# Two transformer layers in one kernel: the first norm in two halves, Q per token tile, two filler banks at the start, wo and w2 loaded later, a margin behind spreads, and the last chunk's waits filled

## The chip, the cores and the metric

The kernel runs on one core of one Trainium2 chip. The core has five engines that run on their own instruction streams and meet through semaphores: TensorE (PE, matrix products into the PSUM banks), VectorE (DVE), ScalarE (ACT), GpSimd (POOL) and SyncE (SP, which here only starts transfers). Each engine takes its own instructions strictly in the order of the program. The metric is the device time of one execution in microseconds (us), lower is better. The time before is the median of three runs, and one more execution was profiled.

## The reference

`x` is 2048 tokens by 512 features in bf16. Two layers are computed, each with the same weights: a block of attention with 32 heads of 16 features, then a dense block with 1792 hidden features.

```python
def _A_ref(x, wqkv, wo):
    B, S, D = x.shape
    H = 32
    Dh = D // H
    qkv = (x @ wqkv).reshape(B, S, 3, H, Dh) ...
    scores = jnp.einsum("bhqd,bhkd->bhqk", q, k) * (Dh ** -0.5)
    p = _softmax(scores, axis=-1)
    o = jnp.einsum("bhqk,bhkd->bhqd", p, v)
    return o ... @ wo

def _B_ref(x, w1, w2):
    h = jnp.einsum("bsd,df->bsf", x, w1)
    h = jnp.maximum(h, zero)
    return jnp.einsum("bsf,fd->bsd", h, w2)

x = A_x
x = x + _A_ref(_layernorm(x, axis=-1), A_wqkv, A_wo)
x = x + _B_ref(_layernorm(x, axis=-1), B_w1, B_w2)
x = x + _A_ref(_layernorm(x, axis=-1), A_wqkv, A_wo)
x = x + _B_ref(_layernorm(x, axis=-1), B_w1, B_w2)
```

## The kernel before, in words

**Tiles.** Tokens are held in 16 tiles of 128 (`x_t`), four to a chunk of 512 queries (`QS`, `TPC`). Heads go in eight groups `t` of four heads, two of them (`e` = 0, 1) to one weight tile `T`. The scores of one head, one key block of 128 (`kb`) and one chunk of queries are one unit: 128 x 512 numbers, one PSUM bank.

**Slots.** The main loop (`while units`) takes three units at a time into the three banks of `ps_s[0]` or `ps_s[1]` in turn. One such step is a slot: three score products on PE (L1583), one exponential on ACT over two or three banks (L1596) into one of five buffers `e`, and later the products with V into `ps_o` (`pv`, L1124). Where the third unit goes to DVE, a piecewise linear stand-in for the exponential is made of one pass per unit (`lin`, L1239) and, for every three such units (a "pair" in the code, `GROUP` = 3), two or three quick passes (`up`, `down`, L1291, L1296). The two together share the work of the softmax; the choice for each slot is made when the program is written, by the conditions in front of `half, take = 0, sg`: room in the buffers, the state of the fillers (`pace`, `press()`), and in the first layer whether V 15 is made, with at most three pairs at a time before that.

**Fillers.** All other products (K, V, Q, the output projection `o`, the dense block's `h` and `z`) are groups in the queues `urgent` and `work`. They run on PE between the slots into one bank, `ps_f` (L511), and DVE empties it (`put_evac`, `do_evac`). `bank_free` is the time at which the bank is free; `fill_pe` starts a group only when nothing waits to be emptied. `owed` and `pace` say how many units of filler a slot may take.

**The order is written out by hand.** The program keeps an estimated clock of PE and DVE in ns (`now_pe`, `now_dve`), of the ends of the exponentials (`exp_end`), of SP's queue (`sp_free`, `sp_lag`) and of POOL (`pool_free`). Every result has an estimated date (`made`, `mark`, `at`), and instructions are put into each engine's stream in the order of these dates. The chip then waits by semaphores for what is really needed. If something comes later than its date, what stands behind it on the same engine waits too.

**The start.** Loads of `x` go out on SP and ACT, of the Q and K weights on SP, ACT and POOL into `stage` (which lies in the later home of `w2`), and are interleaved into `wkq`: T=0 and T=1 by ACT, T=2 and 3 by POOL (L199). 24 idle matmuls (L1317) run on PE. The first four tiles are normed in one go: `ln_stats` (L547), `ln_root` (a reciprocal root by DVE, L568 to L590), `ln_apply` (L598), transposes on PE (L607) and copies (L1345). K, Q and V 0 of the first tile are full-width products (`plain`, L1355), Q is masked into `qbuf` by one DVE pass (L756). `wo` (L224) and `w2` (L1363) are loaded on SP at once, ahead of the DMA transposes of the later chunks (L646), whose landing is dated `CROWDED` = 4500 ns later in the first layer.

**The sums.** A segment of PV products ends in `finish_segment`: DVE copies `ps_o` out (L1016, L1018), SP gathers the row of sums into `c` (L1023), DVE takes reciprocals (L1074), SP scatters them back (L1077) and, except at a chunk's end, POOL's queue spreads them over partitions (L1079); then one product gives `ot`.

**The end.** After the last slot come what is left of PV, the last chunk's projection (L1658), the rest of its `h` groups, a copy of `x` by ACT (L1672), norm, transposes, a copy of `xnT` (L1711), the second-to-last chunk's part of the dense product (`half_part`), the last chunk's dense block (L1749, L1751) and the copy and store of the last tile (L1764, L1765).

```python
need_by = exp_end[no - 1] - MM - PE_TO_ACT
limit = max(need_by - 60.0, s_ready) - SWITCH
...
mark(("c", n, e), lag=sp_lag(SMALL))
```

## Time and profile before

| | us |
|---|---|
| median of three runs | 1464.91 |
| the three runs | 1463.79, 1464.91, 1469.01 |
| the profiled execution | 1468.29 |
| its span, first to last instruction | 1466.5 |
| ACT busy in it | 1431.8 |
| DVE busy in it | 1303.0 |
| PE busy in it | 1373.3 |
| mean granted clock of PE | 0.997 |

The page names engines PE, PEld (weight loads, beside PE), DVE, ACT, POOL and SP; "SPq" and "POOLq" rows are instructions that only start transfers. L12 is line 12 of the kernel. A row of the timeline gives the start, the time from the first to the last of a run of like instructions, engine, line, operation, output and inputs, their number, and in brackets the idle time of the engine before it and what ended that. A row of the groups gives busy time and mean ns of one, then the idle time before. A row of the windows gives the stretch and its length, the busy time of each engine with its instructions, the granted clock, the DMA engines' busy share and GB/s. PE's rows are modelled at their ends, and PE is also given repeated score products to keep it streaming, so its busy share does not say how full it is.

### The profile page before, as it was taken

The page shows a single profiled execution, that of the slowest core. Times are in us where ns is not written, and L with a number is a line of the kernel's source. Part 1 is how long each engine was busy: PE and PEld are TensorE (multiplying, and loading weights), DVE is VectorE, ACT ScalarE, POOL GpSimd, SP SyncE. Part 2 cuts the span into 40 slices and gives each one's busy share as a digit, 9 for nine tenths or more (in the row PEclk, how much of TensorE's full clock was granted, in tenths as well). Part 3 has the DMA queues.
Part 4 walks back from the last instruction along what each step waited for, and adds up shares of the span by engine and source line. Part 5 has one row for each costly group of instructions (what it writes and reads, how often), then busy time and mean ns, then how long its engine had stood idle before and what let it go on. Part 6 is the DMA issues. An engine that isn't in the chain of part 4 may idle for free.

```text
span 1466.5 us, 47730 instructions
## 1 busy us (share of the span) xinstructions
PE 1373.3 (94%) x21066; PEld 511.0 (35%) x21070; DVE 1303.0 (89%) x2409; ACT 1431.8 (98%) x1390; POOL 93.3 (6%) x244
## 2 busy tenths in 40 slices
PE   8899899999999999999899999899999999999998
PEld 3232222222232223322223233223234444545665
DVE  7879999999999999999699977899989599898883
ACT  7999899999999999999999999999999999999996
POOL 4000000001010010000000000001001010010000
PEclk9999899999999999999999999999999999999999
DMA  7101000111012010120100100001111210323120
GB/s 205 19 5 24 18 17 16 42 28 31 10 31 46 13 27 10 38 46 17 24 5 23 34 9 5 11 14 24 39 36 23 46 31 24 72 47 73 21 49 19
DMA packets 135152, 46.59 MB, mean 32 GB/s; under 512 B 119808, under 2 KB 132160, under 8 KB 134944
## 3 DMA queue, kind: packets, MB, share of 16 engines
q1 hardware_dynamic: 128032, 37.47, 10.9%
q0 software_dynamic: 5568, 5.15, 1.9%
q8 instruction: 164, 2.69, 0.8%
q10 hardware_dynamic: 1344, 0.92, 0.2%
q14 instruction: 44, 0.36, 0.1%
HBM read 24.38 MB, written 2.10 MB: 18 GB/s over the span
## 4 chain that ended last, share of the span: by engine, by line
ACT 73%; PE 18%; DVE 6%; issue 2%; DMA 2%; SPq 0%; POOL 0%; DVEq 0%; ACTq 0%
ACT e L1596 72%; PE ps_s L1583 6%; PE ps_f L511 6%; PE ps_o L1124 5%; DVE lin L1239 2%; PE ps_s L1658 1%; DMA wv<-in_A_wqkv_dram 1%; DVE up L1291 0%; DVE down L1291 0%; DMA c<-ht 0%; SPq L224 0%; DVE ht L833 0%; DMA w<-in_B_w_dram 0%; DVE x L872 0%; DVE vaug L742 0%
## 5 line engine op out<-in xcount | busy, mean ns | idle before, releaser
L1596 ACT ACTIVATE e<-ps_s 128x1024 bf16<-128x1024 f32 (+1 forms) x1366 | 1420.3, 1214 | 11.8 <-PE ps_s L1583 9.4
L1239 DVE TENSOR_SCALAR lin<-ps_s 128x512 int16<-128x512 f32 x987 | 659.2, 685 | 42.6 <-PE ps_s L1583 37.0
L1583 PE MATMUL ps_s<-q,ktp 32*128 32x512 bf16 (+2 forms) x6241 | 580.0, 325 | 48.3 <-ACT e L1596 41.3
L1124 PE MATMUL ps_o<-e,vaug 128*32 128x512 bf16 (+2 forms) x4324 | 402.1, 327 | 11.9 <-DVE u L1018 4.4
L1583 PEld LDWEIGHTS <-ktp 32*128 32x128 bf16 x6241 | 183.2, 91 | 520.2 <-issue 503.8
L1124 PEld LDWEIGHTS <-vaug 128*32 128x32 bf16 x7150 | 178.5, 95 | 236.2 <-issue 205.1
L1291 DVE TENSOR_SCALAR up<-lin 128x1536 int16<-128x1536 int16 x329 | 181.2, 551 | 10.1 <-PE ps_o L1124 9.3
L1291 DVE TENSOR_SCALAR down<-lin 128x1536 int16<-128x1536 int16 x329 | 181.4, 552 | 2.0 <-PE ps_o L1124 1.9
L1124 PE MATMUL ps_o<-up,vaug 128*32 128x512 bf16 (+2 forms) x1308 | 170.1, 329 | 0.0
L1124 PE MATMUL ps_o<-lin,vaug 128*32 128x512 bf16 (+2 forms) x1308 | 155.5, 328 | 2.2 <-DVE ktp L993 1.0
L1124 PE MATMUL ps_o<-down,vscaled 128*32 128x512 bf16 (+2 forms) x1098 | 142.6, 335 | 3.3 <-DVE down L1291 2.9
L511 PE MATMUL ps_f<-xnT,w 128*32 128x512 bf16 (+2 forms) x2080 | 135.2, 343 | 5.0 <-DVE ht L833 3.8
L511 PE MATMUL ps_f<-w,ht 128*32 128x512 bf16 x1680 | 128.9, 382 | 0.9 <-DVE ht L833 0.5
L511 PE MATMUL ps_f<-xnT,wkq 128*32 128x512 bf16 (+2 forms) x1376 | 99.2, 352 | 7.6 <-DVE ktp L706 1.6
L833 DVE TENSOR_SCALAR ht<-ps_f 128x512 bf16<-128x512 f32 (+1 forms) x108 | 73.0, 676 | 23.8 <-PE ps_f L511 23.7
L511 PEld LDWEIGHTS <-w 128*32 128x32 bf16 x2080 | 46.9, 95 | 43.6 <-issue 33.8
L1124 PEld LDWEIGHTS <-vscaled 128*32 128x32 bf16 x1098 | 45.9, 96 | 19.1 <-issue 13.0
L511 PEld LDWEIGHTS <-ht 128*32 128x32 bf16 x1680 | 37.0, 95 | 40.0 <-issue 25.4
L511 PEld LDWEIGHTS <-wkq 128*32 128x32 bf16 x1376 | 32.4, 95 | 39.9 <-issue 31.7
L547 DVE BATCH_NORM_STATS2 stats<-x 128x6 f32<-128x512 bf16 x64 | 42.7, 684 | 2.5 <-ACT x L1672 1.1
L511 PE MATMUL ps_f<-wv,xnT 128*32 128x512 bf16 x496 | 37.7, 382 | 5.7 <-DVE vaug L742 2.2
L511 PE MATMUL ps_f<-wo,ot 128*32 128x512 bf16 x496 | 39.7, 382 | 0.8 <-DVE x L794 0.5
(139 smaller groups left out, 537.8 us busy)
## 6 DMA issues: line engine op xcount, KB each, us to landing
w<-in_B_w_dram SPq DMA_DIRECT2D x130, 128.0 KB
q<-xn SPq DMA_DIRECT2D x48, 64.0 KB
out_dram<-x SPq DMA_DIRECT2D x16, 128.0 KB
x<-in_A_x_dram SPq DMA_DIRECT2D x14, 128.0 KB
w<-in_B_w_dram SPq DMA_DIRECT2D x1, 1792.0 KB
u<-r POOLq DMA_DIRECT2D x12, 128.0 KB, 4.5
ktp<-in_B_w_dram SPq DMA_DIRECT2D x10, 128.0 KB
u<-ht POOLq DMA_DIRECT2D x6, 128.0 KB, 4.5
```

The source lines that it names most:

```text
L511: nc.tensor.matmul(out[cols], lhsT[:, cols], rhs, start=i % k == 0, stop=i % k == k - 1, tile_position=(0, 32 * g), skip_group_check=True,)
L547: nc.vector.bn_stats(out=stats[ln_n(tag)][:, i, :], in_=x_t[tt][:])
L833: nc.vector.tensor_scalar(out=out, in0=sums, scalar1=0.0, scalar2=None, op0=ALU.max)
L1124: nc.tensor.matmul(ps_o[32 * g : 32 * g + 32, 0 : sg["w"]], values[:, 4 * sg["T"] + g, 2 * e : 2 * e + 32], rhs, start=g not in sg["begun" ...
L1239: first = nc.vector.tensor_scalar(out=lin[which][:, half * QS : (half + 1) * QS], in0=src, scalar1=EXP_BIAS, scalar2=0.0, op0=ALU.add, op1 ...
L1291: nc.vector.tensor_scalar(out=out, in0=line, scalar1=by, scalar2=0.0, op0=ALU.add, op1=ALU.max)
L1583: score = nc.tensor.matmul(b[:, a : a + sg["w"]], kt[32 * g : 32 * g + 32, kc : kc + P], qbuf[sg["n"] % 2][32 * g : 32 * g + 32, sg["e"], ...
L1596: ex = nc.scalar.activation(out=eb[:, 0 : place[m]], in_=b[:, 0 : place[m]], func=ACTF.Exp, scale=1.0 / (LOG2E * UNIT),)
L1658: uses(nc.tensor.matmul(out, lhsT, rhs, start=first, stop=last), b, needs=needs)
```

## The change

- **Norm and Q at the start.** The first norm runs in two halves of two tiles; the root is one power on POOL per half, the same form that the end of the kernel uses. The transposed tiles go to fixed banks. K is made for 128 and then for 384 columns, Q by tile of 128 tokens into one bank, its masks by two passes. The idle matmuls are 13, then 4 and 3 between the halves. V 0 becomes a filler like V 1 to 3.
- **Weights.** Of the interleaves of T=0 and T=1 all but Q's T=0 move from ACT to POOL. `wo` and `w2` wait in a queue `to_load` and go out one per slot from slot 30, when the estimate has SP free, `w2` in 14 pieces. Dates are written in for `wkq`, `wv` and the tiles of `x`, and groups and statistics depend on them.
- **Two filler banks.** Until the first PV product `ps_o` serves as a second bank for fillers, and PV starts once `BOTH` = 4 exponentials are pending and no filler is open.
- **Margins.** The landing of `c` is dated `BEHIND` = 3500 ns later while a spread is under way. `CROWDED` holds only before 18000 ns. The estimated clocks start 2760 ns (PE) and 3100 ns (DVE) sooner.
- **The end.** Before the last PV, fillers and PV are placed in the waits for the last two exponentials. Statistics of the last tile are read from PSUM beside ACT's copy. The transposes go to `ps_o`'s bank first, `xnT` is copied by DVE and ACT in halves, and the last tile is copied and stored in halves on two queues.

```diff
-    CROWDED, POOL_ISSUE = 4500.0, 700.0
+    CROWDED, POOL_ISSUE, BEHIND = 4500.0, 700.0, 3500.0
+    LOADED, FIRST_LOAD = 18000.0, 30
+    BOTH = 4
+    X_AT = (9.9, 10.1, 11.0, 11.4, 11.6, 11.9, 12.2, 12.5, 13.5, 14.5, 15.0, 15.5)
+    WQ_AT, WV_AT = {0: 0.0, 1: 12500.0, 2: 16500.0, 3: 17900.0}, 9900.0
...
+    to_load = deque()
     for T in range(NDC):
         for e in range(2):
             rows = A_wo[T * P : (T + 1) * P, :].rearrange("(g e d) f -> e g d f", g=4, e=2)
-            nc.sync.dma_start(out=wo[1 - e : P : 2, T, :], in_=rows[e])
+            to_load.append((wo[1 - e : P : 2, T, :], rows[e]))
+    for ft in range(NF):
+        to_load.append((w2[:, ft, :], B_w2[ft * P : (ft + 1) * P, :]))
...
+    def next_bank():
+
+        if not two[0] or any(e[3] == 1 for e in evac):
+            return 0
+        if any(e[3] == 0 for e in evac):
+            return 1
+        return int(bank_free[1] < bank_free[0])
+
     def start_group(g):
         (urgent if g in urgent else work).remove(g)
-        ready = max(at(g["deps"], "pe"), bank_free[0] + DVE_TO_PE)
+        now_bank[0] = next_bank()
+        ready = max(at(g["deps"], "pe"), bank_free[now_bank[0]] + DVE_TO_PE)
...
-                if evac:
+                if len(evac) > two[0]:
                     return
...
-                lag = sp_lag(TRANSPOSE) + (0.0 if l else CROWDED)
+                lag = sp_lag(TRANSPOSE) + (CROWDED if now_dve[0] < LOADED else 0.0)
...
-                mark(("c", n, e), lag=sp_lag(SMALL))
+                behind = BEHIND if now_dve[0] < spread_till[0] else 0.0
+                mark(("c", n, e), lag=sp_lag(SMALL) + behind)
...
                 lag = max(pool_free[0] - now_dve[0] + SPREAD_LAG, R_LAG)
+                spread_till[0] = now_dve[0] + lag
...
+            if two[0] and (len(pend) < BOTH or cur or evac):
+                break
...
-    idle_matmuls(24)
+    idle_matmuls(13)
...
+    for n in range(2):
+        rows = range(n * HALF, (n + 1) * HALF)
+        for i in rows:
+            ln_stats(tag, i, i)
+        for i in rows:
+            nc.vector.bn_aggr(out=mv[0][:, i, :], in_=stats[0][:, i, :])
+        nc.vector.tensor_scalar(
+            out=half_va[n][:], in0=mv[0][:, rows.start : rows.stop, 1], scalar1=EPS, scalar2=None,
+            op0=ALU.add,
+        )
+        nc.gpsimd.tensor_tensor(
+            out=half_ya[n][:], in0=half_va[n][:], in1=masks[:, 4:5].to_broadcast((P, HALF)),
+            op=ALU.pow,
+        )
+        set_ones(*((8, 13), (13, 16))[n])
+    interleave(nc.gpsimd.tensor_copy, 0, 0)
+    interleave(nc.gpsimd.tensor_copy, 0, 1)
+    set_ones(16, len(ones))
+    interleave(nc.gpsimd.tensor_copy, 1, 1)
...
+    for n in range(2):
+        for i in range(n * HALF, (n + 1) * HALF):
+            head_apply(i)
+        for i in range(n * HALF, (n + 1) * HALF):
+            head_transpose(i)
+        idle_matmuls((4, 3)[n])
+    interleave(nc.scalar.copy, 1, 0)
+    head_k(0, P, (2, 0))
     for i in range(TPC):
...
+        head_q(i)
+    head_k(P, QS, (0, 1))
...
-    now_pe[0] = 13160.0
-    now_dve[0] = 14500.0
-    exp_end = {-1: 12600.0, 0: 13600.0}
+    now_pe[0] = 10400.0
+    now_dve[0] = 11400.0
+    exp_end = {-1: 9900.0, 0: 10900.0}
+    pool_free[0] = WQ_AT[3]
+    sp_free[0] = 15500.0
...
+        if to_load and no >= FIRST_LOAD and sp_free[0] < now_pe[0]:
+            out, in_ = to_load.popleft()
+            nc.sync.dma_start(out=out, in_=in_)
+            sp_lag(W1, "pe")
+    assert not to_load
+    owed[0] = 99.0
+    for limit in (exp_end[slot[0] - 1], exp_end[slot[0]]):
+        fill_v(limit, 1)
+        fill_pe(limit + ACT_TO_PE)
...
-    more = [(last, w) for w in range(W)] + [(3, 0)]
+    more = [(3, 0)] + [(last, w) for w in range(W)]
...
+        uses(
+            nc.vector.bn_stats(out=stats[ln_n(tag)][:, i, :], in_=at_bank(banks[i])), banks[i], "x"
+        )
         uses(nc.scalar.copy(out=x_t[tt + i][:], in_=at_bank(banks[i])), banks[i], "x")
...
-        copy = nc.vector.tensor_copy if i % 2 else nc.scalar.copy
-        uses(copy(out=xnT[NQS - 1][:, :, part(i)], in_=pt), more[i], "xnT")
+        for n, copy in enumerate((nc.vector.tensor_copy, nc.scalar.copy)):
+            cs = slice(n * NDC // 2, (n + 1) * NDC // 2)
+            uses(copy(out=xnT[NQS - 1][:, cs, part(i)], in_=pt[:, cs]), more[i], "xnT")
...
+        for copy, queue, a in ((nc.scalar.copy, nc.scalar, 0), (nc.vector.tensor_copy, nc.sync, D // 2)):
+            cols = slice(a, a + D // 2)
+            uses(copy(out=x_t[tt + i][:, cols], in_=at_bank(banks[i])[:, cols]), banks[i])
+            queue.dma_start(
+                out=out_flat[(tt + i) * P : (tt + i + 1) * P, cols], in_=x_t[tt + i][:, cols]
+            )
```

143 lines of the change are left out of this document (82 added, 61 removed).

## The prediction

> **What bounds the kernel now.** I read the page first, then ACT's waits, then three stretches of the timeline: the start, the one long gap of ACT, the end.
>
> ```profile
> span 1466.5 us, 47730 instructions
> PE 1373.3 (94%) x21066; PEld 511.0 (35%) x21070; DVE 1303.0 (89%) x2409; ACT 1431.8 (98%) x1390; POOL 93.3 (6%) x244
> ...
> L1596 ACT ACTIVATE e<-ps_s 128x1024 bf16<-128x1024 f32 x987 | 931.3, 1097 | 7.6 <-PE ps_s L1583 5.7 <-PE ps_o L1124 0.7
> L1596 ACT ACTIVATE e<-ps_s 128x1536 bf16<-128x1536 f32 x378 | 530.7, 1519 | 4.2 <-PE ps_s L1583 3.6 <-PE ps_o L1124 0.2
> ```
>
> ACT is busy for 98% of the span, nearly all in the exponentials of L1596. There are 987 + 378 + 1 = 1366 slots, one ACTIVATE each. The idle column holds 11.8 us in all. A slot takes three score blocks of 512 columns, and in 987 of them DVE takes the third, so ACT reads 1024 columns and not 1536. The two mean times differ by 0.422 us: a block more for DVE saves ACT that much. So four things can change the time: when the first exponential starts, gaps between exponentials, the number of DVE blocks, and what follows the last exponential.
>
> The start (timeline, 0 to 25 us, and SP's next row after it):
>
> ```profile
> 1.18 8.27 PE L1317 MATMUL ps_o<-e 128*128 128x512 bf16 x24 [1.18 <-DVE e L207]
> 3.31 2.47 DVE L547 BATCH_NORM_STATS2 stats<-x 128x6 f32<-128x512 bf16 x4 [0.92 <-DMA x<-in_A_x_dram]
> 5.70 0.36 DVE L568 BATCH_NORM_AGGREGATE mv<-stats 128x2 f32<-128x6 f32 x4
> 7.13 1.83 PEld L1317 LDWEIGHTS <-e 128*128 128x128 bf16 x9 [0.28 <-issue]
> 7.58 1.39 ACT L199 COPY wkq<-w 128x512 bf16<-128x512 bf16 x2 [4.43 <-DMA w<-in_A_wqkv_dram]
> 8.20 1.38 DVE L598 TENSOR_SCALAR xn<-x,mv,ya 128x512 bf16<-128x512 bf16 x4
> 10.59 0.86 DVE L1345 COPY xnT<-ps_s 128x512 bf16<-128x512 bf16 x2 [1.01 <-PE ps_s L607]
> 11.60 1.89 PE L1355 MATMUL ps_s<-xnT,wkq 128*128 128x512 bf16 x7 [0.18 <-DVE xnT L1345]
> 13.53 1.23 DVE L756 TENSOR_TENSOR q<-ps_s,masks 128x1024 bf16<-128x1024 f32 x1 [0.88 <-PE ps_s L1355]
> 15.24 1.45 ACT L1596 ACTIVATE e<-ps_s 128x1536 bf16<-128x1536 f32 x1 [0.72 <-PE ps_s L1583]
> 19.58 1.07 POOL L564 TENSOR_TENSOR ya<-va,masks 128x4 f32<-128x4 f32 x1
> 23.93 24.60 SPq L646 DMA_TRANSPOSE xnT<-xn  x12
> ...
> 97.09 1.19 SPq L779 DMA_DIRECT2D q<-xn  x2
> ```
>
> Four statistics, a reciprocal root by DVE steps (6.1 to 8.2), four scalings, transposes, K, Q, its masks and the first scores stand in one chain of 15.24 us. On SP twelve transposes follow, and nothing from 48.5 to 97.
>
> The long gap (timeline, 141 to 160 us, and windows):
>
> ```profile
> 141.44 1.38 POOL L1079 DMA_DIRECT2D u<-ht  x2 [110.31 <-DVE ht L1016]
> 141.94 0.59 SPq L1023 DMA_DIRECT2D c<-ht  x1
> 147.22 0.35 DVE L1074 RECIPROCAL c<-c 128x32 f32<-128x32 f32 x1 [3.01 <-DMA c<-ht]
> 148.04 0.61 PE L1124 MATMUL ps_o<-down,vscaled 128*32 128x512 bf16 x3 [2.87 <-DVE down L1291]
> 149.67 1.02 ACT L1596 ACTIVATE e<-ps_s 128x1024 bf16<-128x1024 f32 x1 [2.90 <-PE ps_s L1583]
> ...
> 156.81 43.85 ACT L1596 ACTIVATE e<-ps_s 128x1024 bf16<-128x1024 f32 x44 [0.49 <-PE ps_s L1583]
> ...
> 140.00:160.00 20.00, 16.27 (x139) 3.59 (x138) 14.70 (x27) 15.08 (x16) 2.60 (x4) 0.74 0.22 43
> ```
>
> The 8 KB copy of the sums was issued 0.5 us after two 128 KB spreads on POOL's queue, and its RECIPROCAL started 5.3 us after the issue. DVE takes its work in order, so it stood 3.0 us before the reciprocal; behind it stood `down`, for that PE, and for PE ACT 2.9 us. Then the granted clock falls (0.74 over the window) and ACT waits 0.49 to 0.50 us before each of the next slots. In this window ACT is busy 15.08 of 20: 4.9 us lost.
>
> **The change, part by part.**
>
> *First norm.* The order written out: statistics of tiles 0, 1, their aggregate and eps, statistics of 2, 3, the same; the root is one POW on POOL per half; DVE's nine small steps go. From the rows: 3.31 + 2.47 + 0.36 + two eps steps (some 0.3 each with their gaps) = 6.75. The second POW ends at about 7.6: 1.07 for four columns here, 0.57 for one (end, below), I take 0.75 for two. Tiles 0 and 1 are scaled in that wait, 2 and 3 by 8.35, against 9.58 before: 1.2 us sooner. Ahead of the POWs on POOL stand eight memsets, and the K weights of T=0 follow behind them (copy 0.7, as ACT's 1.39 for two), ready at about 8.7, before the first K needs them.
>
> *Q per token tile.* Transposes to 9.3 with four idle matmuls between the pairs, last copy (0.43) to 9.8. K of the first 128 columns, Q by 16 matmuls of 128 columns, K of the other 384: the row of seven 512-column matmuls gives 0.27 each; 128 columns cost 0.07 by width and 0.14 if weight loads limit, so Q 1.1 to 2.2. Half masks follow (half of 1.23). First scores wait for the first mask only, but the copy of K's 384 columns (about 0.5) stands ahead of the first exponential on ACT. That gives 12.6 to 13.7; I take 13.1, a gain of 2.1. Bounds: 1.5 from the slow end, and 2.8, the distance between the start times that the scheduler is given (13160 and 10400 ns).
>
> *Weights of T=1.* Two ACT copies (1.38, done before 15.24) go to POOL, which the program waits for by a date; 0 on ACT.
>
> *Idle matmuls.* Row 7.13: the loads come after an idle of 0.28 up to there (0.43 apart with the load's own 0.15), and nine in 1.83 us from there, 0.20 apart, so the first 13 end at about 6.8, with 0.4 us to the first transpose. The Trainium skill (TensorE: Matmul & The Clock Gate, "Part 1: The HAM clock gate") says that the array starts at half clock and is released after a busy window of about 3.4 us which runs free of the kernel. By it thirteen are enough, unless the window falls badly; the trace agrees in kind (0.43, then 0.20) and shows the change of pace 5.9 us after the first matmul.
>
> *Loads moved.* SP loses eight wo issues and the 1.8 MB w2 before the transposes, so w1 and the transposes meet an emptier queue; 22 smaller issues come one per slot from slot 30. SP is free from 48.5 to 97.09, and slots 30 to 60 fall in about 50 to 90; the 22, at the 0.6 of the copy of 141.94, are 13 us of that: 0. With the cover gone each late transpose would cost at most its own 0.6.
>
> *Two filler banks, first PV held until four exponentials are pending, transposes believed sooner.* Here is the supply of DVE blocks.
>
> ```profile
> 20.00:40.00 20.00, 16.74 (x215) 5.15 (x211) 13.30 (x25) 19.30 (x15) 6.28 (x19) 1.00 0.80 186
> ...
> 70.00:80.00 10.00, 1.96 (x3) 1.00 0.01 2
> ...
> 102.92 0.79 DVE L742 CAST vaug<-ps_f 128x512 bf16<-128x512 f32 x1 [2.01 <-PE ps_f L511]
> ...
> 110.00:120.00 10.00, 7.55 (x12) 1.00 0.01 2
> ```
>
> (The 10 us windows are of L1239 alone.) Before the sixteenth V is evacuated, at 103.7, pairs are held to three at a time, 3 blocks in 10 us; after it, 12. Sooner V brings the fast stretch forward. But the bank lasts only until the first PV, some five slots, and the norms of chunks 1 to 3 wait for POOL as before (its clock starts at 17900 for them), so I expect V 15 some 4 us sooner beside the shift of the start, and 3 blocks more: 1.3 us. Ends: 3 blocks fewer (-1.3) and 10 more (4.2). The held PV is made up in PE's 3.3 us of slack in 20 to 40.
>
> *Margin behind spreads.* The reciprocal is planned 3.5 us later when a spread is under way. 5.3 us after the issue is 5.9 after the DVE step that released it; the planned lag becomes about 0.2 + 0.6 + 1.45 + 3.5 = 5.75. What is left of the wait is 0.1, and what DVE does instead is ready work. The gap goes: 4.8. Late next is the spread, which has the 10 us of its own date. Ends: 0, if it returns elsewhere, and 4.9.
>
> *The end* (timeline, 1429 us on, and one early row for a price; the last exponential ends at 1429.73 + 16.87 = 1446.6):
>
> ```profile
> 35.52 0.69 DVE L706 CAST ktp<-ps_f 128x512 bf16<-128x512 f32 x1 [0.48 <-PE ps_f L511]
> ...
> 1429.73 16.87 ACT L1596 ACTIVATE e<-ps_s 128x1536 bf16<-128x1536 f32 x13
> 1442.96 0.42 DVE L833 TENSOR_SCALAR ht<-ps_f 128x256 bf16<-128x256 f32 x1
> 1449.24 0.59 ACT L1672 CAST x<-ps_s 128x512 bf16<-128x512 f32 x1 [2.64 <-PE ps_s L1658]
> 1449.86 0.69 DVE L547 BATCH_NORM_STATS2 stats<-x 128x6 f32<-128x512 bf16 x1 [1.10 <-ACT x L1672]
> 1451.03 0.57 POOL L1699 TENSOR_TENSOR ya<-va,masks 128x1 f32<-128x1 f32 x1 [24.67 <-DVE va L1695]
> 1452.48 0.38 PE L607 MATMUL ps_s<-ident,xn 128*128 128x128 bf16 x4 [0.48 <-ACT ht L831]
> 1452.91 3.19 PE L1658 MATMUL ps_s<-w,ht 128*128 128x512 bf16 x14
> 1462.85 0.59 ACT L1764 CAST x<-ps_s 128x512 bf16<-128x512 f32 x1 [0.63 <-PE ps_s L1658]
> 1463.46 0.33 SPq L1765 DMA_DIRECT2D out_dram<-x  x1
> ```
>
> Statistics straight from PSUM drop the copy from the chain: 0.6, if they read PSUM as fast (DVE's 512-column read of PSUM in row 35.52 takes 0.69, as the statistics from SBUF do here). The transposes' own bank drops the wait for `ht`, 0.48. But four `h` groups also run in that wait, and PE takes them first: filled earlier, the whole 1.1 is had; left there, 0.5. The halved xnT copy is worthless while the fourteen matmuls of 1452.91 stand ahead on PE. The last copy in halves: 0.59 to 0.42, two queues: 0.2. Sum 1.0 to 1.3, or 0.5 at the low end; I take 1.2.
>
> **Sum.** 2.1 + 1.3 + 4.8 + 1.2 = 9.4 us. The profiled execution took 1468.29 (span 1466.5 and 1.8 around it); less 9.4 is 1458.9. The median of the runs is 1464.91 (1463.79, 1464.91, 1469.01): less 9.4 is 1455.5. Part of the 3.4 between them may be the gap itself, smaller in some runs; the order of the two queues that makes it is fixed by the program, so I stay near the second: 1456.
>
> **Rivals.**
>
> *The gap is moved, or small in the unprofiled runs.* For it: two runs at 1464, two at 1469, about a gap apart; every slot is laid out anew, and the next spread can catch another transfer. Against it: the margin holds wherever a spread is dated. Then 9.4 - 4.8 = 4.6 remain: 1460.3. Chance 0.25.
>
> *The array stays slow in the head.* If the gap between the thirteen matmuls and the transposes spoils the release, the head's PE work of some 2.5 us doubles: 1458.5. This is the rule of the skill read against the change; the row of 7.13 speaks against it, as the release falls only 0.3 after the thirteenth. Chance 0.07.
>
> *DVE blocks lost* (the other side).
>
> ```profile
> 700.00:720.00 20.00, 17.17 (x220) 5.67 (x216) 9.41 (x19) 20.00 (x17) 1.33 (x3) 1.00 0.15 28
> 720.00:740.00 20.00, 18.86 (x223) 6.12 (x222) 18.60 (x38) 20.00 (x21) 0.00 (x0) 1.00 0.05 16
> ```
>
> The scheduler's gates on the backlog close at times: DVE drops to 9.41 of 20, and ACT gets 17 slots through, not 21: 4 slots, 3.8 us. All gates stand on the same estimated clock, which the change moves. More such droughts eat the gain: the 9.4 are gone at 22 blocks lost (22 x 0.422), and four droughts more (15 us) give 1470.5. For it: such droughts exist before. Against it: nothing in the change adds DVE work after the head. Chance 0.1.
>
> *Blocks won.* V early and one drought less, 15 blocks more than my three: 6.3 us, 1450. For it: DVE is busy 13.3 of 20 in row 20:40. Against it: two fillers at once last five slots. Chance 0.13.
>
> **How the numbers follow.** Forecast 0.45, rivals 0.25, 0.07, 0.1, 0.13. 0.5% is 7.3 us, about what a measurement of this kernel can tell from no change, so the line to faster is 1457.6. The forecast's own range, 1452.5 to 1459.5 by the ends above, lies some three quarters below it: 0.34, with the blocks won 0.13, and of the moved gap and the slow array, whose prices spread over 3 us, about 0.07: faster 0.54. Slower needs over 1472: 0.07, within the fourth rival's spread. Same 0.39. The range reaches to the moved gap and into the lost blocks above, and to the blocks won below: 1449 to 1465.
>
> **What would show it.** First exponential at 13.1 (not below 12.4, not above 13.7). Granted clock 1.00 and ACT 20 of 20 throughout 120 to 180. V 15 evacuated before 98. The count of 1024-column exponentials 987 to 997. From the last exponential's end to the last store's issue 15.7 where 16.8 stood. The forecast is wrong if a new gap of ACT above 1 us appears, if the count falls under 975, or if the gap of 149.67 turns up under another transfer.

## The result and the profile after

The changed kernel took 1457.13 us, the median of 4 runs (1456.49 to 1457.35), against 1465.74 of the kernel before run beside it (1463.79 to 1469.01). The ratio is 0.9938, 95% interval [0.9919, 0.9957]: 8.6 us less, where 9.4 had been forecast and 1456 named. The profiled execution of the changed kernel took 1457.35 us. The page's first lines:

```profile
span 1455.5 us, 47936 instructions
PE 1367.1 (94%) x21143; PEld 508.9 (35%) x21143; DVE 1310.0 (90%) x2421; ACT 1424.9 (98%) x1389; POOL 97.0 (7%) x249
```

The groups of ACT's exponentials, by form (count, then total and mean, then the idle time ahead of them):

```profile
L1678 ACT ACTIVATE e<-ps_s 128x1024 bf16<-128x1024 f32 x996 | 938.8, 1098 | 3.1 <-PE ps_s L1665 1.6 <-PE ps_o L1144 0.8
L1678 ACT ACTIVATE e<-ps_s 128x1536 bf16<-128x1536 f32 x369 | 520.2, 1514 | 3.2 <-PE ps_s L1665 2.0 <-PE ps_o L1144 0.5
```

Nine blocks more went to DVE (996 for 987), and the idle time ahead of the exponentials fell from 11.8 to 6.3 us. Third, ACT's rows of the timeline and the window that held the long gap:

```profile
14.00 4.26 ACT L1678 ACTIVATE e<-ps_s 128x1536 bf16<-128x1536 f32 x3 [0.19 <-PE ps_s L1665]
...
21.62 661.25 ACT L1678 ACTIVATE e<-ps_s 128x1536 bf16<-128x1536 f32 x655 [0.35 <-PE ps_o L1144]
...
1418.78 16.75 ACT L1678 ACTIVATE e<-ps_s 128x1536 bf16<-128x1536 f32 x13 [0.40 <-PE ps_s L1665]
```

```profile
140.00:160.00 20.00, 17.82 (x206) 5.68 (x202) 19.20 (x37) 20.00 (x21) 1.38 (x2) 1.00 0.11 22
```

The first exponential starts at 14.00 instead of 15.24. From 21.62 on, 655 exponentials stand in one row, without a gap that the view would split; ACT is busy 20.00 of 20 between 140 and 160, at a granted clock of 1.00. The last one ends at 1418.78 + 16.75 = 1435.53, and the span ends 19.97 later.

So the difference of the two spans, 11.0 us, splits like this:

| | before | after | less by |
|---|---|---|---|
| first exponential starts | 15.24 | 14.00 | 1.24 |
| ACT idle between exponentials (first start to last end, less their busy time) | 11.1 | 6.0 | 5.0 |
| exponentials, busy | 1420.3 | 1415.5 | 4.8 |
| last exponential's end to the span's end | 19.9 | 19.97 | -0.07 |

The profiled execution of before was one of its longer ones (1468.29; the runs begin at 1463.79), so these 11.0 us hold 2.4 more than the medians do. Which parts of the change the rows belong to is what the experiments had to say.

### The profile page after: what moved, and what is told of

The parts are those of the page before. It is cut to its first block, busy times and chain, and to the rows that moved or that the text cites. A ratio compares the mean times of both kernels' runs of the same rounds, so it can differ in the third digit from the quotient of the medians.

```text
span 1455.5 us, 47936 instructions
## 1 busy us (share of the span) xinstructions
PE 1367.1 (94%) x21143; PEld 508.9 (35%) x21143; DVE 1310.0 (90%) x2421; ACT 1424.9 (98%) x1389; POOL 97.0 (7%) x249
## 4 chain that ended last, share of the span: by engine, by line
ACT 70%; PE 21%; DVE 7%; issue 2%; DMA 1%; POOL 0%; DVEq 0%; ACTq 0%; SPq 0%
ACT e L1678 70%; PE ps_f L526 7%; PE ps_s L1665 7%; PE ps_o L1144 6%; DVE lin L1264 2%; PE ps_s L1749 1%; DVE up L1316 1%; DVE down L1316 0%; DVE ht L851 0%; DVE x L890 0%; DVE stats L562 0%; DVE down L1321 0%; DVE xn L1390 0%; PE ps_f L622 0%; DVE vaug L758 0%
## 5 line engine op out<-in xcount | busy, mean ns | idle before, releaser
L1678 ACT ACTIVATE e<-ps_s 128x1024 bf16<-128x1024 f32 (+1 forms) x1366 | 1415.5, 1210 | 6.3 <-PE ps_s L1665 3.6
L526 PE MATMUL ps_f<-xnT,wkq 128*32 128x512 bf16 (+2 forms) x1376 | 96.0, 353 | 5.2 <-DVE ht L851 1.3
L571 POOL TENSOR_TENSOR ta<-stats 128x4 f32<-128x4 f32 (+2 forms) x17 | 4.7, 275 | 575.5 <-DVE stats L562 575.5
```

The lines of the kernel that those rows point to most:

```text
L526: nc.tensor.matmul(out[cols], lhsT[:, cols], rhs, start=i % k == 0, stop=i % k == k - 1, tile_position=(0, 32 * g), skip_group_check=True,)
L571: pool.tensor_tensor(out=t1, in0=st[:, :, 1], in1=st[:, :, 4], op=ALU.subtract)
L1678: ex = nc.scalar.activation(out=eb[:, 0 : place[m]], in_=b[:, 0 : place[m]], func=ACTF.Exp, scale=1.0 / (LOG2E * UNIT),)
```

## The experiments

Each is an edit of the changed kernel unless it says otherwise. Several chips were used, on which the kernel before had medians of 1464.77 to 1467.10, so parts are compared by their ratio to the kernel before run beside them; 0.001 is 1.47 us. Each ratio is known to 0.001 to 0.002, so a difference of two ratios below some 0.002 (3 us) isn't clear of noise by itself; where a part is smaller than that, the rows of its traces have to show it.

### The start: POOL beside the scalings

The first exponential came 0.9 later than the 13.1 forecast. The timeline of the changed kernel, 6 to 11 us:

```profile
6.61 0.73 DVE L1390 TENSOR_SCALAR xn<-x,mv,half_ya 128x512 bf16<-128x512 bf16 x2
6.78 0.79 POOL L1373 TENSOR_TENSOR half_ya<-half_va,masks 128x2 f32<-128x2 f32 x1 [0.39 <-DVE half_va L1369]
...
7.61 2.81 DVE L1390 TENSOR_SCALAR xn<-x,mv,half_ya 128x512 bf16<-128x512 bf16 x2 [0.27 <-POOL half_ya L1373]
...
7.71 1.52 POOL L203 COPY wkq<-w 128x512 bf16<-128x512 bf16 x2
...
9.13 1.13 POOL L239 MEMSET vaug<- 128x32 bf16 x12
...
10.48 0.40 PE L622 MATMUL ps_s<-ident,xn 128*128 128x128 bf16 x4 [1.41 <-DVE xn L1390]
```

The statistics and both POWs came as forecast (0.73 and 0.79 for the 0.75 taken). But the second pair of scalings took 2.81 us where the first took 0.73, and it ran beside two copies and twelve memsets of POOL. In the kernel before POOL's memsets ended at 6.55 and the scalings began at 8.20. The last transposes waited 1.41 us for it. The experiment holds POOL back until the scalings are done, by a copy of one column of `xnbuf[3]`:

```diff
-    interleave(nc.gpsimd.tensor_copy, 0, 0)
-    interleave(nc.gpsimd.tensor_copy, 0, 1)
-    set_ones(16, len(ones))
...
         idle_matmuls((4, 3)[n])
+    nc.gpsimd.tensor_copy(out=warm[:], in_=xnbuf[TPC - 1][:, 0:1])
+    interleave(nc.gpsimd.tensor_copy, 0, 1)
+    interleave(nc.gpsimd.tensor_copy, 1, 1)
+    set_ones(16, len(ones))
...
+    interleave(nc.scalar.copy, 0, 0)
     interleave(nc.scalar.copy, 1, 0)
```

> The changed kernel, with POOL's copies and the last twelve memsets held until the fourth scaling (a one-column POOL copy that reads it), and K's T=0 weights interleaved by ACT after its two transposed copies. Theory (the third and fourth scalings of the first norm took 1.00 and 1.89 us in the changed kernel, where two others took 0.37, because POOL's copies and memsets ran beside them): all four scalings 0.35 to 0.45 us, first exponential at 12.7 to 13.2 us where it was 14.00, time about 1456.0 (1.1 us less). Rival (what stretched them is something else, such as the loads that land at 350 GB/s): scalings stay at 1.0 and 1.9, and the first exponential comes at 14.0 to 14.7, later for the copy given to ACT.

Measured: 1456.06 us (1455.41 to 1456.25, 4 runs), ratio 0.9935 [0.992, 0.995]. Its timeline:

```profile
7.47 0.36 POOL L239 MEMSET vaug<- 128x32 bf16 x3
7.55 0.74 DVE L1382 TENSOR_SCALAR xn<-x,mv,half_ya 128x512 bf16<-128x512 bf16 x2 [0.27 <-POOL half_ya L1373]
...
12.29 2.92 ACT L1678 ACTIVATE e<-ps_s 128x1536 bf16<-128x1536 f32 x2 [0.19 <-PE ps_s L1665]
```

With the copies and the twelve memsets out of the way the same two scalings take 0.74, and the first exponential starts at 12.29, 1.71 sooner, even before the band of the theory. The span fell by 1.4 (1454.1); the ratio moved by only 0.0003, which is inside the noise. So POOL's copies and memsets, which the prediction had laid beside the head at no cost, took back more than half of what the head could have gained (1.71 of 2.95). Which of the two does it isn't parted. Three memsets still ran beside the first of these scalings (row of 7.47) and didn't stretch it, which speaks for the copies.

The Trainium skill (SBUF — State Buffer, "SBUF: two separate sides") says that GpSimd shares one pair of ports with VectorE, and that a GpSimd instruction and a VectorE instruction in a two-port mode lock each other out: whichever begins first holds the pair to its end. Here the trace agrees in part: the second scaling ended at 10.42, just behind the memsets (9.13 + 1.13). But the first of the pair began at 7.61, ahead of the first copy (7.71), and was stretched all the same. Nor does every POOL instruction lock DVE out: the scalings of 6.61 ran beside a POW and took 0.73, and that of 7.55 beside memsets.

### The second filler bank

First, one bank from the start, which also takes away the hold on the first PV:

```diff
-    two = [True]
+    two = [False]
```

> The changed kernel with one filler bank throughout (two is False from the start, so PV is not held for four exponentials either). Theory (the second bank is what makes V sooner and so gives DVE blocks): the sixteenth V is evacuated 2 to 5 us later than 99.97, DVE takes 987 to 992 blocks and not 996, and the time is 1458.5 to 1461. Rival (the blocks come from the dates of the transposes, or from the layout by chance): 994 or more blocks, the sixteenth V within 1 us, the time within 1 us of 1457.

Measured, in one run: 1464.87 us, 987 blocks. The blocks are as the theory had them, the time lies above its band. Second, the hold stays and only the bank goes:

```diff
     def next_bank():
 
-        if not two[0] or any(e[3] == 1 for e in evac):
-            return 0
-        if any(e[3] == 0 for e in evac):
-            return 1
-        return int(bank_free[1] < bank_free[0])
+        return 0
...
-                if len(evac) > two[0]:
+                if evac:
```

> The changed kernel with PV still held until four exponentials are pending, but with ps_f as the only filler bank. It parts the two edits that the run with one bank (1464.87, 987 blocks) took away together. If the second bank is what counts: 985 to 990 blocks, a gap of ACT over 1 us near 30 us, 1462 to 1465. If the hold of PV counts (fillers run first, PV later): 993 or more blocks, no such gap, 1456.5 to 1459.

Measured, in one run: 1461.67 us, 987 blocks again. It's the bank that counts for the blocks; what the hold is worth can't be told from one run each. DVE's passes over the blocks in the first three windows of 50 us (DVE busy and count, granted clock, DMA share, GB/s), first the changed kernel, then this one:

```profile
0.00:50.00 50.00, 4.14 (x7) 1.00 0.49 120
50.00:100.00 50.00, 17.94 (x28) 1.00 0.15 48
100.00:150.00 50.00, 28.01 (x43) 1.00 0.11 24
```

```profile
0.00:50.00 50.00, 2.06 (x3) 1.00 0.50 121
50.00:100.00 50.00, 16.02 (x24) 1.00 0.15 45
100.00:150.00 50.00, 24.91 (x38) 1.00 0.10 22
```

Why a bank that is in use for a few slots does this can be seen in the evacuations of V. The changed kernel, DVE's timeline:

```profile
16.46 0.76 DVE L758 CAST vaug<-ps_f 128x512 bf16<-128x512 f32 x1
...
17.70 0.77 DVE L758 CAST vaug<-ps_o 128x512 bf16<-128x512 f32 x1
...
99.20 0.77 DVE L758 CAST vaug<-ps_f 128x512 bf16<-128x512 f32 x1
```

and with the hold but one bank:

```profile
16.43 0.76 DVE L754 CAST vaug<-ps_f 128x512 bf16<-128x512 f32 x1
18.85 0.77 DVE L754 CAST vaug<-ps_f 128x512 bf16<-128x512 f32 x1
...
105.00 0.77 DVE L754 CAST vaug<-ps_f 128x512 bf16<-128x512 f32 x1
```

With one bank V follows V at 2.4 us, since PE waits for DVE and DVE for PE; with two, at 1.24. PE ends the fourth V of the first chunk at 20.1 with two banks and at 24.0 with one, and the later fillers move up with it: the sixteenth V comes 5.8 us sooner. How 3.9 us become 5.8 on the way wasn't followed. ACT also has a gap of 1.44 us at 29.48 with one bank, which the changed kernel doesn't have; the same gap of 1.44 stands in all four traces with one bank:

```profile
29.48 31.25 ACT L1674 ACTIVATE e<-ps_s 128x1536 bf16<-128x1536 f32 x27 [1.44 <-PE ps_s L1661]
```

Because this was larger than forecast and stood on single runs, the last kernel was run again, timed:

> The changed kernel with one filler bank again, now in several runs. Theory (the second bank is worth some 4.5 us): 1460.8 to 1462.5, that is 0.9965 to 0.998 of the kernel before run beside it where the changed kernel stood at 0.9938; 987 blocks to DVE. Rival (the single look fell badly, the bank is worth 2 us or less): under 1459.5.

Measured: 1462.34 us (1461.47 to 1465.67, 10 runs), ratio 0.9972 [0.9963, 0.9982]. The bank is worth 0.9972 - 0.9938 = 0.0034, some 5.0 us, with an interval of about 2 to 8 by the two ratios. Of it 9 blocks x 0.422 = 3.8 and the gap 1.4 are seen in the traces.

### Loads of wo and w2

They go back to the start, everything else stays:

```diff
-            to_load.append((wo[1 - e : P : 2, T, :], rows[e]))
-    for ft in range(NF):
-        to_load.append((w2[:, ft, :], B_w2[ft * P : (ft + 1) * P, :]))
+            nc.sync.dma_start(out=wo[1 - e : P : 2, T, :], in_=rows[e])
...
+    nc.sync.dma_start(out=w2[:], in_=B_w2[:, :].rearrange("(c p) f -> p c f", p=P))
     mark(("k", 0, 0, 0))
```

> The changed kernel with wo and w2 loaded on SP at the start, ahead of the transposes, as the kernel before has them; the dates stay. Theory (w2 ahead of the transposes is what made the time of before vary, by a wait that the one profile shows as 0.4 us and the margin's run as 4.0): the scalings wait 0.5 to 4 us for transposes again, ACT has a gap of 0.5 to 3 us between 22 and 45 us, the runs lie over 2.5 us apart, the median is 1458.5 to 1463. Rival (the transposes were no bound, the loads were moved for nothing): 1456.5 to 1457.8 and runs within 1.2 us.

Measured: 1459.48 us (1459.24 to 1461.97, 5 runs), ratio 0.9959 [0.9946, 0.9972]. ACT's longest gap in its timeline, then DVE's waits between 20 and 45 us (total, times, longest):

```profile
35.39 1.45 ACT L1677 ACTIVATE e<-ps_s 128x1536 bf16<-128x1536 f32 x1 [1.66 <-PE ps_s L1664]
```

```profile
DVE xn L611 <- DMA xnT<-xn: 1.6, 1, 1.6
```

DVE stands 1.6 us in front of a scaling, because the buffer that it writes is still being read by a DMA transpose that lies behind the load of 1.8 MB. Behind it stand an evacuation and then the scores. In the changed kernel this row isn't there. The profiled execution is the longest of the five, so the others may have waited less. The loads were costed at 0; moving them is worth 0.0021, 3.1 us by the ratios and 2.35 by the medians. The ratios alone don't clear the noise, but all five runs lie above all four of the changed kernel, as the theory had it.

Then both are undone, the bank and the loads, which leaves the head, the margin and the tail:

> The changed kernel with one filler bank and with wo and w2 loaded at the start, so that of its parts the earlier start, the margin and the tail are left. Theory (the parts add: the bank some 4.5, the loads some 2.4): 1463.0 to 1465.5, 0.998 to 1.000 of the kernel before run beside it; a gap of ACT of 1.5 to 3 us at 28 to 42 us. Rival (they overlap: late transposes also starve the second bank, so that what the bank gives hangs on the loads having been moved): within 1 us of the one bank alone, 1461 to 1462.5.

Measured: 1466.31 us (1461.75 to 1469.61, 10 runs), ratio 0.9997 [0.9987, 1.0007]. The parts add up as the theory says, by the ratio; in microseconds it came 0.8 above the theory's band, beside a kernel before that stood at 1466.44. Beside one bank the loads are worth 0.9997 - 0.9972 = 0.0025, 3.7 us, and here the two intervals don't touch. The gap of 1.5 to 3 us that the theory wanted isn't in the trace, which is of the quickest of the ten runs (1461.75): DVE waited 0.8 us for a transpose there, and ACT has only the gap of one bank. What is left, head, margin and tail together, is worth 0.4 us, between -1.0 and 1.9. And its ten runs scatter over 7.9 us, as the nineteen of the kernel before do (1463.24 to 1469.78 beside it), where the ten with one bank and late loads lie within 4.2 and the changed kernel's four within 0.9.

### The margin

Without it, in the changed kernel:

```diff
-    CROWDED, POOL_ISSUE, BEHIND = 4500.0, 700.0, 3500.0
+    CROWDED, POOL_ISSUE, BEHIND = 4500.0, 700.0, 0.0
```

> The changed kernel with BEHIND = 0, all else as it is. Theory (the margin removed the long gap): within 120 to 180 us ACT loses 2 to 5 us again, the granted clock of that stretch falls below 1.00, a RECIPROCAL waits 1 us or more for a copy of sums issued behind two spreads, and the time is 1459 to 1462. Rival (the shift of the whole layout took the copy of sums away from the spread): ACT is busy 19.9 or more of 20 in each window there, and the time is 1457 as with the margin.

Measured: 1456.65 us (1456.1 to 1457.77, 4 runs), ratio 0.9941 [0.9926, 0.9956]. The rival held. The gap doesn't come back, and the two kernels do the same at this place. SP's row in the changed kernel, which without the margin is the same but 0.01 sooner:

```profile
128.76 9.42 SPq L1041 DMA_DIRECT2D c<-ht  x2
```

The row holds two copies of sums, the first issued at 128.76, the second at 137.6, so that it ends at 138.2. POOL's two spreads started at 129.12, so in the new layout of the slots the second copy comes 8.5 us after them, where in before 0.5 us lay between. Its RECIPROCAL starts at 142.92 in the one kernel and 142.91 in the other, and DVE doesn't wait for it. It was the layout that took the wait away. The run without the margin has 993 blocks where the changed kernel has 996, so even such an edit moves the layout by 3.

The other half of the question is the margin alone, in the kernel before (the same three lines of `behind` and `spread_till` as in the change):

> The kernel before with the margin alone: the landing of the sums is dated 3500 ns later while a spread is under way. Theory: the gap of 147 to 157 us is gone, ACT's idle time before the exponentials falls from 11.8 to about 7, the tail and the start stay (first exponential 15.24), the time is 1460.5 to 1462, and the runs lie within 1.5 us where those of before spread over 5.2. Rival (the gap moves to another transfer or was small in most unprofiled runs): 1463.5 to 1466.

Measured: 1468.73 us (1466.81 to 1470.47, 10 runs), ratio 1.0018 [1.0005, 1.003]: slower. ACT and DVE in its timeline, then a window:

```profile
32.23 0.41 DVE L599 TENSOR_SCALAR xn<-x,mv,ya 128x512 bf16<-128x512 bf16 x1 [3.60 <-DMA xnT<-xn]
...
35.45 1.45 ACT L1599 ACTIVATE e<-ps_s 128x1536 bf16<-128x1536 f32 x1 [2.21 <-PE ps_s L1586]
```

```profile
140.00:160.00 20.00, 17.48 (x192) 5.12 (x185) 19.98 (x38) 20.00 (x23) 2.60 (x4) 1.00 0.17 34
```

The margin did what it says: ACT is busy 20.00 of 20 between 140 and 160. But this execution had the wait behind the loads, 3.60 us at 32.23, at a place where its program is the same as before's, which had 0.4 there. And it had 984 blocks, 3 fewer (1.3 us). The expectation was missed. Nor is it only that wait: five of the ten runs show a mean granted clock of 1.000 and still took 1466.81 to 1468.31. What else the margin costs there isn't traced.

### Half clock without a stall

The one bank ran in two profiled executions of the same program, at 1461.67 and 1465.67 us. PE's waits up to 150 us are alike in both. The windows (PE, PEld, DVE, ACT, POOL busy; granted clock, DMA share, GB/s), first the quick one, then the other:

```profile
148.00:150.00 2.00, 1.53 (x16) 0.47 (x16) 2.00 (x4) 2.00 (x4) 1.09 (x2) 1.00 0.20 31
150.00:152.00 2.00, 1.53 (x16) 0.38 (x16) 1.97 (x5) 2.00 (x4) 0.00 (x0) 1.00 0.48 92
```

```profile
148.00:150.00 2.00, 1.53 (x16) 0.47 (x16) 2.00 (x5) 2.00 (x4) 0.94 (x2) 1.00 0.25 42
150.00:152.00 2.00, 1.94 (x16) 0.36 (x16) 1.97 (x4) 1.85 (x3) 0.00 (x0) 0.54 0.45 86
...
162.00:164.00 2.00, 2.00 (x23) 0.48 (x19) 0.94 (x2) 1.10 (x1) 0.00 (x0) 0.54 0.04 4
```

and PE's timeline in the second:

```profile
148.23 0.61 PE L1661 MATMUL ps_s<-q,ktp 32*128 32x512 bf16 x6 [0.53 <-ACT e L1674]
...
150.06 0.98 PE L1661 MATMUL ps_s<-q,ktp 32*128 32x512 bf16 x6 [0.31 <-ACT e L1674]
```

The same six score products take 0.61 us and then 0.98. The means of 0.54 at both ends, over 2 us each, say that the granted clock was at half from about 150.2 to about 163.8; the windows between them show 0.50. In the quick execution every window from 140 to 168 shows 1.00. ACT, busy throughout in the quick execution, lost 3.0 us between 140 and 168 in the other, most of the 4.0 between the two. PE had waited for nothing longer than 0.53 us in the six microseconds ahead; it had little to do, 1.53 us of 2. What set it off in one execution and not in the other stays open.

The Trainium skill (TensorE: Matmul & The Clock Gate, "Part 1: The HAM clock gate") has the array fall back to half clock after an idle window of about 3.4 us. No wait of that length stands ahead of this fall, so the trace doesn't agree with that as it is worded.

How often this happens can be read from the mean granted clock that is on record for each execution; as the windows show either 1.00 or 0.50 and their mixtures, 0.001 of it stands for some 2.9 of 1466 us at half clock, an estimate. Of the ten runs of this program nine have 0.999 or 1.000 (1461.47 to 1463.49 us) and one 0.995 (1465.67). Of the fifty of the kernel before that were run beside the experiments, ten have 0.999 and took 1463.19 to 1464.38 us, and eighteen have 0.995 or less and took 1466.00 to 1471.34. So most executions of the kernel before lose time at half clock, and how much they lose sets most of their scatter. The changed kernel's four all show 1.000.

### The end

The forecast had 1.2 us here; the profile shows none. The changed kernel, timeline from 1437 us on, and its last rows:

```profile
1437.33 0.35 DVE L1067 SCALAR_TENSOR_TENSOR ot_last<-ps_o,masks,r 128x128 bf16<-128x128 f32 x1
...
1437.74 0.39 PE L1749 MATMUL ps_s<-wo,ot_last 128*128 128x512 bf16 x1 [0.59 <-DVE ot_last L1067]
...
1438.23 0.70 DVE L1766 BATCH_NORM_STATS2 stats<-ps_s 128x6 f32<-128x512 f32 x1 [0.55 <-PE ps_s L1749]
1438.96 0.59 ACT L1768 CAST x<-ps_s 128x512 bf16<-128x512 f32 x1 [3.44 <-DVE stats L1766]
...
1440.01 0.41 DVE L613 TENSOR_SCALAR xn<-x,mv,ya 128x512 bf16<-128x512 bf16 x1 [0.68 <-POOL ya L1793]
1440.16 0.63 PE L526 MATMUL ps_s<-xnT,ktp 128*32 128x128 bf16 x32 [1.48 <-ACT ht L849]
...
1441.84 0.40 PE L622 MATMUL ps_o<-ident,xn 128*128 128x128 bf16 x4
...
1442.29 3.19 PE L1749 MATMUL ps_s<-w,ht 128*128 128x512 bf16 x14
...
1451.93 0.37 ACT L1860 CAST x<-ps_s 128x256 bf16<-128x256 f32 x1 [0.64 <-PE ps_s L1749]
...
1452.33 0.42 DVE L1860 CAST x<-ps_s 128x256 bf16<-128x256 f32 x1 [1.47 <-ACT x L1860]
1452.79 0.33 SPq L1861 DMA_DIRECT2D out_dram<-x  x1
```

The statistics read PSUM in 0.70, as forecast, and the chain of the norm is shorter: `xn` is ready at 1440.42, 4.89 after the last exponential, where before it was 5.45. But ACT's copy of the same bank had to wait for the statistics (3.44 idle, released by DVE), so it comes 0.73 later, and behind it on ACT stand the `relu` evacuations of the open `h` groups. PE takes these groups ahead of the transposes and waits 1.48 for ACT. So the transposes start 1441.84 - 1435.53 = 6.31 after the last exponential; before it was 1452.48 - 1446.60 = 5.88. That is 0.43 lost, and the rest of the way, from the fourteen matmuls on, is 0.38 shorter (13.59 before, 13.21 now). The halved last copy has no part in that: its halves run one after the other, DVE's released by ACT's, and from the copy's start to the last store's issue it takes 0.86, where the whole copy took 0.61. What is shorter is the way from the fourteen matmuls to that copy (9.64 for 9.94) and from the last store's issue to the span's end (2.71 for 3.04).

Two experiments. One leaves the last two waits unfilled:

```diff
     assert not to_load
-    owed[0] = 99.0
-    for limit in (exp_end[slot[0] - 1], exp_end[slot[0]]):
-        fill_v(limit, 1)
-        fill_pe(limit + ACT_TO_PE)
```

> The changed kernel without the fill of the waits for the last two exponentials. Theory (the fill puts an h group on PE whose evacuation then stands on ACT behind the copy of x, and that delays the groups ahead of the transposes): from the last exponential's end to the span's end 19.0 to 19.6 us where it was 19.97. Rival (the fill is worth its group): 20.2 to 20.8 us.

Measured, in one run: 1458.53 us, span 1456.8. The last exponential ends at 1435.91, the rest takes 20.89: a hair above the rival's band of 20.2 to 20.8. The fill is worth 0.9; it doesn't cause the loss.

The other empties the open group at once, runs two `h` groups while DVE makes the last root, and puts half of the second-to-last chunk's dense product ahead of the transposes:

```diff
     while cur:
         do_piece()
+    while evac:
+        do_evac()
+    for _ in range(2):
+        g = next(g for q in (urgent, work) for g in q if at(g["deps"], "pe") is not None)
...
+        start_group(g)
+        while cur:
+            do_piece()
+        do_evac()
...
+    half_part(0, range(NF // 2))
...
-    half_part(0, range(NF))
+    half_part(0, range(NF // 2, NF))
```

> The changed kernel with another order at the end: the open h group is evacuated at once, two h groups run in the wait for the last root, ahead of the last projection, and the first half of the second-to-last chunk's dense product runs ahead of the transposes, the second half behind them. Theory (the transposes and the dense product stand behind PE's h groups, these behind ACT's copy, that behind the statistics of the same bank): transposes 4.9 to 5.3 us after the last exponential's end where they came at 6.3, from there to the span's end 17.0 to 17.8 us where it was 19.97, time 1454.2 to 1455.0. Rival (the last chunk's dense block or the stores bound the end): 19 us or more, time above 1456.

Measured: 1455.89 us (1455.43 to 1456.56, 4 runs), ratio 0.9935 [0.9921, 0.9948]; the end takes 18.24, 1.73 less, though not the 17.0 to 17.8 of the theory, and the time lies between the two bands. The ratio moved by 0.0003, inside the noise, so the gain is read from the trace. Its timeline:

```profile
1437.86 0.35 DVE L1067 SCALAR_TENSOR_TENSOR ot_last<-ps_o,masks,r 128x128 bf16<-128x128 f32 x1
...
1438.73 0.63 PE L526 MATMUL ps_s<-xnT,ktp 128*32 128x128 bf16 x32 [0.49 <-ACT ht L849]
1439.29 0.39 PE L1749 MATMUL ps_s<-wo,ot_last 128*128 128x512 bf16 x1
...
1440.85 1.67 PE L1749 MATMUL ps_s<-w,ht 128*128 128x512 bf16 x7
...
1442.36 0.39 PE L622 MATMUL ps_o<-ident,xn 128*128 128x128 bf16 x4
```

The second of the two early groups waited for ACT and put off the last projection to 1439.29, 1.08 us after `ot_last` was ready (1437.86 + 0.35); in the changed kernel it began 0.06 after it. The transposes came no sooner, 6.30 after the last exponential (1436.06). What was gained is that seven matmuls and not fourteen stand behind them, 1.67 us for 3.19: 1.5 of the 1.7.

### Both additions together

> The changed kernel with POOL held until the fourth scaling (the first experiment) and the other order at the end (the one before this). Theory: the two gains add, 1.1 and 2.5: time 1453.0 to 1454.0. Rival (the sooner start is given back in the layout, or the end was bound elsewhere): 1455 or more.

Measured: 1454.02 us (1453.09 to 1454.61, 5 runs), ratio 0.9921 [0.9909, 0.9934]. By the spans start and end add up: 1.4 and 1.2 less alone, 2.8 less together (1452.7). The ratios (0.0003, 0.0003 and 0.0017 less than the changed kernel's) are too coarse to show it.

With one early `h` group in place of two:

> As the kernel with both (POOL held, other order at the end), with one h group in the wait for the last root and not two. In the kernel with the other order alone the second early group waited 0.49 us for ACT's evacuation of the first and put the last projection off from 1438.25 to 1439.29. Theory: the projection comes 2.2 us after the last exponential's end and not 3.2, the end from there takes 17.2 to 17.7 us where it was 18.24, and the time is 1453.0 to 1453.6. Rival (the group not run early stands ahead of the transposes again): no gain, 1454.0 to 1454.6.

Measured: 1454.99 us (1454.36 to 1455.61, 5 runs), ratio 0.9916 [0.9902, 0.993], span 1452.6 for 1452.7. No difference: its last exponential ended 0.47 sooner, and the rest took 18.65 for 18.3, since three groups were left to run ahead of the transposes. The projection did come 2.2 after the last exponential, as the theory had it, but nothing was won behind it. These two versions are the quickest found, and which of them is quicker isn't shown; they beat the changed kernel by about 2.5 to 3 us.

## Why the prediction was right, and where its steps were not

The time was 1.1 us off, and well inside the range. But the sum came out right over terms that were not. Head, margin and end were forecast 7 us too high together, the bank and the loads some 6 to 7 us too low, and that the two cancel is luck:

| term of the forecast | forecast | what the runs showed |
|---|---|---|
| earlier first exponential | 2.1 | 1.24 (trace) |
| DVE blocks and two banks | 1.3 | 5.0 (ratios; traces 3.8 + 1.4) |
| loads moved | 0 | 2.4 to 3.1 beside two banks, 3.7 beside one |
| margin and long gap | 4.8 | 0 for the margin in the new layout |
| end | 1.2 | -0.07 |
| whole change (forecast: the sum; measured: the medians) | 9.4 | 8.6 |

*First norm and Q.* The mechanism was right, the size off, and 14.00 lies above the 13.7 named as the bound. What was mis-sized is the step "tiles 2 and 3 by 8.35": they were scaled by 10.42. The row used for a scaling came from a stretch where POOL was silent, and the change had moved POOL's copies and memsets into just that stretch. With POOL held the first exponential came at 12.29, better than the 13.1, so the rest of the head was costed too high: from the last copy's end (9.62) it took 2.67 where 3.3 had been named.

*Idle matmuls.* Thirteen were enough; the loads of weights come closer together from 4.96 us on. That rival fell.

*Two banks.* "The bank lasts only some five slots, so 3 blocks more" mis-sized the term by nearly four times. V 15 was evacuated at 99.97, not before 98, so even the visible sign was smaller than named, and yet 9 blocks came of it and a gap of 1.4 us that one bank has. Few slots were enough because with one bank each V of the first chunk waits for the evacuation of the one ahead of it.

*Loads.* "SP is free from 48.5 to 97.09: 0" was right for the new place of the loads, and no cost showed there. What failed is that it priced the old place at nothing too. In the trace of before the wait of DVE for the transposes was 0.4 us, and the forecast went by that one execution; in other kernels with the load at that place it was 0.8, 1.6 and 3.6.

*Margin.* "The gap goes: 4.8" was right of the place and wrong of the cause. The gap went without the margin, because the slots were laid out anew; and the margin alone took the gap away and made the kernel no quicker. The step that failed is "the order of the two queues that makes it is fixed by the program". The order is, the loss isn't: of two executions of one program one fell to half clock for 13.6 us at this very stretch, the other didn't. Before's profiled execution held 4.9 us there, and its best runs (1463.19) lie 5.1 below that execution. The granted clock of the fifty runs above bears that out: its ten best show 0.999, which leaves room for some 3 us at half clock where the profiled execution spent some 10 at this stretch. No trace of such a run was taken, so whether the wait itself goes there too is left open.

*End.* Each of the three parts was there, but "filled earlier, the whole 1.1 is had" failed: the copy of `x` came to stand behind the statistics, and the `h` evacuations behind the copy. The 0.2 for the last copy failed too: its two halves run in turn and take 0.25 more.

*Rivals.* "The gap is moved, or small in the unprofiled runs" was half true: the margin's term did fall out. It was made good by the bank and the loads, which is "blocks won" in part. DVE blocks were not lost.

*The signs.* Of those named, the granted clock (1.00 in 120 to 180), ACT's share there (59.93 of 60) and the count (996) came. The first exponential (14.00), V 15 (99.97) and the way from the last exponential to the last store's issue (17.26 for 15.7) did not. And a new gap of ACT above 1 us, which the forecast had named as a sign of being wrong, did appear, at a place that nobody had watched and where the trace of before has none above 0.6:

```profile
1363.33 10.19 ACT L1678 ACTIVATE e<-ps_s 128x1024 bf16<-128x1024 f32 x11 [1.18 <-PE ps_s L1665]
```

The traces of the kernels that only change the start or the end have at most 0.76 at this place, so part of it belongs to this execution. Its cause is open.

What the change bought is thus of two kinds. In the best runs it is the bank and the start: the best run with one bank and early loads is 1461.75, before's 1463.19, the changed kernel's 1456.49. The rest is evenness: the changed kernel's runs keep within 0.9 us.

## What to carry to other kernels

Before a sum is made from one profiled execution, it has to be asked of each wait whether the program or the run made it; a wait behind a DMA queue or a half clock is worth its mean over runs, which one trace can't show. Work that is moved to an "idle" engine has to be checked for the port, the bank or the queue that it shares with the critical one, with the row of the neighbour that runs beside it. Where products and their evacuations take turns in one bank, a second bank for a few slots can be worth more than those slots, as everything queued behind moves up; here it was 9 blocks. And one has to go back to the signs that the forecast named, over the whole length of the trace, when the time comes out right.

## What the runs showed of the hardware that was not expected

- Two bf16 scalings of 128x512 took 0.73 us beside a POW of POOL, 0.74 beside three memsets, and 2.81 beside two copies and twelve memsets.
- The granted clock went to half for about 13.6 us with no wait of PE over 0.53 us ahead of it, in one of two traced executions of the same program; ACT lost 3.0 us by it. The mean granted clock of that program's ten runs shows such a fall in one.
- Two engines that read one PSUM bank ran one after the other: ACT's copy started 0.03 us after the end of DVE's statistics, and DVE's half of the last copy 0.03 after ACT's. In both the profile names the other engine as what released it, so it is an order that the program keeps; what two readers at once would do no run shows.
- A DMA transpose queued behind a load of 1.8 MB held up DVE for 0.4, 0.8, 1.6 or 3.6 us, in four executions of four kernels with the load at the same place.
